# A one-core transformer block: values in 128-token matmuls, swapped by small DMAs, and a new written-out order

## The chip, the cores and the metric

The kernel runs on one core of one Trainium2 chip. Its time is the device time of one execution, in microseconds, and the profile's span is the time from the first to the last instruction of one profiled execution. Engines are named as in the profile: PE is TensorE (PEld its weight loads), DVE VectorE, ACT ScalarE, POOL GpSimd, and SP the engine that issues nearly all DMAs.

## The reference

Activations x are 2048 tokens by 512 features, in bfloat16. A conditioning vector c (1 x 512) gives, by `silu(c) @ w_mod`, six modulation vectors of 512 (sa, ca, ga, sb, cb, gb). Then:

```
h = layernorm(x) * (1 + ca) + sa
x = x + ga * attention(h)              # 32 heads of 16; a token sees itself and the 255 before it
h = layernorm(x) * (1 + cb) + sb
g = layernorm(h)                       # then an MLP across tokens, not features:
u = gelu(g^T (512 x 2048) @ w1 (2048 x 1792) + b1)
x = x + gb * (u @ w2 (1792 x 2048) + b2)^T
```

## The kernel before, in words

**Tiles and groups.** The tokens are 16 tiles of 128 (`xres`), worked on in four groups G of 512 tokens. For each group `proj` normalizes x (`norm_ops`, `normalize`), transposes it to h1T (features on the partitions; group 0 by PE, groups 1 to 3 by DMA transposes that SP issues, line 825), applies the modulation, and makes queries, keys and values with `wqkv`. A head has only 16 features, so scores are made for 4 heads by 32 rows of PE, with two heads of one 32-row strip kept apart by zeros: GpSimd multiplies each key tile twice with a parity mask (`kk`, KT).

**Chunks.** `attention(group)` runs over 75 chunks of at most 512 score columns for each of four row strips. One chunk is scores (S, on PE, into the PSUM tiles `pss` of three banks and `psb` of one), two exponentials on ACT (EA of 1536 columns, EB of 512, into `et`), a mask on DVE, and then, by units of 256 queries, AV: et times the values VT, and et times ones for the denominators. ACT takes the logarithm and exponential of the denominators (`lz`), DVE multiplies (`OT`). Group 0 has chunks 0 to 14, the others 20 each.

**Values.** VT holds, per block of 64 tokens and per head, 64 + 64 partitions by 32 columns: even heads' values on the first 64 partitions in the first 16 columns, odd heads' on the last 64 in the last 16, zeros elsewhere. In groups 0 (line 754) and 1 to 3 (line 907) one tile of 128 tokens is two half tiles of eight matmuls. Each matmul takes 64 tokens as the weights and 256 value columns (the even or the odd heads) and writes 64 output partitions; even and odd go to different columns of PE's array, so that the result already lies on the right partitions. It is copied once to `vb` (`e_ve`), and GpSimd writes it twice into VT, each time with a half mask that makes the zeros (`e_vp`, line 938).

**First queries.** `opening` (line 671) makes the first 256 tokens' keys and queries of the first 8 heads. The keys of tokens 0 to 127 and the queries share a PSUM tile of three banks (`box["warm"]`) that earlier held warm-up matmuls and next holds the first scores; DVE and ACT read them from there (`e_split`, line 691).

**MLP.** `post` finishes a group: output projection (pa), second and third layer norm, hb. `partials` (line 1034) multiplies the first eight hb tiles (groups 0 and 1) with w1 and puts 14 partial sums aside (pu, `part`), as filler on PE; the first four parts stand in a pool of their own, the later ones in room that the projections give back. `tail` does the rest of MLP1, gelu and guT; the loop at line 1302 then makes 16 output tiles: 14 matmuls into py, one addition on DVE (`otile`), one DMA.

**What sets the order.** Every step is an `op` with an engine, a planned cost and dependencies. `ORDER` (line 59) is the order of all 1,112 steps, written out by hand as a list of numbers; `CHOSEN` says which engine takes a step that can go to more than one. `run_schedule` (line 152) emits the steps in that order; the costs only decide which of three PSUM banks (`ps_od`) a step takes. Each engine, and SP's DMA queue, then works strictly in its own part of that order, and semaphores do the waiting. Since all goes through the recording class at line 225, nearly every instruction in the profile has line L233, and they are told apart by their tiles.

Of the kernel before, what the change touches and what calls it, by code (L numbers as in the profile page):

```python
# [25 lines left out]
NPART = 14  # L26
PART_AT = 20.0
# [3 lines left out]
X_READY = [3.0, 3.6, 11.8, 12.2]  # L31
MOD_READY = [4.7, 5.4, 6.2, 6.9]
W_READY = [8.1, 8.95, 8.95, 11.4, 13.6]
# [20 lines left out]
SWITCH = 0.095  # L54
LATENCY = {"PE": 0.18, "ACT": 0.15, "DVE": 0.13, "POOL": 0.15, "SP": 0.0}
# [4 lines left out]
    38, 3, 1, 9, 39, 4, 10, 11, 2, 12, 40, 13, 7, 0, 41, 6, 14, 16, 42, 17, 43, 44, 45, 18, 46, 47, 19, 8, 20, 5,  # L60
    48, 49, 51, 50, 52, 53, 55, 54, 56, 69, 57, 70, 121, 71, 122, 73, 72, 74, 58, 75, 79, 76, 123, 125, 59, 80, 77,
    126, 84, 81, 78, 85, 82, 83, 127, 129, 88, 60, 86, 130, 61, 87, 62, 63, 66, 124, 64, 67, 89, 65, 68, 133, 90,
    131, 92, 134, 259, 93, 91, 105, 94, 106, 260, 135, 137, 107, 97, 95, 138, 261, 98, 108, 96, 262, 139, 161, 110,
    99, 162, 263, 111, 109, 101, 132, 163, 140, 165, 102, 166, 112, 136, 141, 114, 142, 264, 103, 143, 169, 167,
    115, 128, 144, 100, 116, 170, 145, 146, 481, 120, 147, 151, 117, 148, 266, 179, 15, 171, 152, 119, 149, 168, 21,
    268, 267, 180, 22, 482, 113, 150, 269, 153, 23, 183, 181, 27, 118, 154, 28, 184, 265, 155, 24, 270, 182, 156,
    172, 104, 157, 185, 271, 29, 193, 25, 158, 164, 194, 30, 186, 31, 26, 159, 32, 197, 195, 173, 273, 160, 198,
    174, 483, 175, 187, 272, 188, 176, 201, 199, 484, 189, 177, 202, 485, 274, 178, 703, 275, 278, 203, 276, 211,
    279, 212, 704, 281, 280, 282, 277, 204, 190, 215, 213, 285, 283, 216, 286, 200, 284, 289, 214, 191, 196, 319,
    217, 290, 192, 287, 320, 205, 486, 705, 293, 488, 487, 37, 321, 323, 291, 206, 324, 288, 36, 207, 297, 218, 298,  # L70
    706, 208, 327, 325, 294, 299, 328, 300, 219, 295, 220, 209, 33, 337, 35, 329, 221, 210, 338, 34, 301, 707, 330,
    927, 489, 302, 225, 222, 303, 341, 339, 928, 226, 322, 223, 342, 228, 224, 229, 340, 490, 326, 304, 343, 230,
    351, 292, 305, 352, 227, 234, 306, 331, 237, 353, 492, 355, 231, 356, 354, 296, 232, 238, 235, 929, 344, 357,
    359, 236, 332, 360, 307, 493, 333, 233, 308, 239, 309, 361, 369, 491, 708, 334, 311, 310, 370, 312, 240, 345,
    313, 241, 371, 373, 346, 335, 494, 374, 930, 347, 336, 315, 495, 316, 375, 383, 348, 503, 317, 384, 242, 504,
    358, 496, 314, 362, 349, 387, 385, 497, 350, 505, 388, 363, 376, 244, 364, 365, 372, 931, 389, 391, 506, 498,
    507, 366, 392, 390, 500, 318, 709, 243, 501, 393, 401, 246, 502, 508, 367, 402, 386, 377, 710, 378, 509, 379,
    245, 712, 403, 405, 511, 380, 368, 406, 510, 404, 932, 519, 394, 512, 407, 415, 713, 520, 513, 499, 416, 250,
    395, 396, 521, 417, 419, 714, 408, 381, 397, 420, 515, 382, 248, 247, 516, 421, 249, 423, 517, 933, 523, 398,
    424, 251, 526, 527, 422, 715, 524, 425, 528, 433, 522, 399, 711, 426, 434, 409, 410, 525, 411, 400, 412, 529,  # L80
    252, 437, 435, 530, 438, 418, 531, 253, 427, 514, 532, 428, 439, 541, 436, 413, 429, 440, 542, 533, 414, 254,
    534, 716, 537, 430, 535, 545, 543, 538, 431, 546, 441, 432, 442, 540, 717, 443, 544, 257, 547, 539, 549, 447,
    444, 548, 550, 255, 448, 450, 256, 449, 451, 551, 559, 459, 536, 718, 445, 560, 719, 446, 452, 453, 552, 561,
    258, 563, 456, 460, 564, 457, 518, 720, 454, 458, 565, 573, 553, 455, 574, 554, 461, 733, 575, 462, 577, 734,
    578, 566, 463, 722, 735, 723, 579, 581, 724, 725, 582, 576, 555, 580, 726, 562, 583, 591, 464, 727, 737, 556,
    592, 738, 584, 466, 567, 739, 593, 595, 465, 568, 557, 596, 729, 558, 468, 467, 569, 721, 597, 472, 605, 730,
    606, 469, 740, 473, 470, 570, 609, 607, 731, 741, 728, 610, 474, 585, 586, 471, 571, 613, 736, 611, 587, 572,
    594, 614, 755, 475, 742, 476, 588, 623, 615, 598, 756, 624, 744, 757, 745, 616, 599, 625, 627, 589, 600, 628,
    479, 590, 601, 612, 747, 480, 608, 629, 746, 637, 748, 477, 602, 630, 638, 617, 626, 478, 618, 749, 619, 639,
    743, 641, 631, 603, 632, 642, 604, 633, 935, 732, 620, 645, 643, 936, 621, 937, 646, 622, 758, 938, 640, 940,  # L90
    644, 647, 939, 655, 941, 656, 648, 750, 942, 943, 657, 659, 649, 634, 658, 660, 650, 944, 651, 751, 635, 763,
    661, 636, 752, 764, 662, 946, 753, 947, 948, 652, 754, 765, 767, 949, 653, 768, 663, 654, 664, 950, 665, 769,
    771, 669, 666, 770, 772, 670, 672, 671, 673, 667, 781, 773, 668, 951, 674, 782, 678, 766, 679, 774, 675, 783,
    785, 680, 676, 786, 681, 952, 784, 775, 677, 787, 795, 776, 796, 788, 777, 759, 682, 760, 778, 799, 797, 953,
    761, 762, 800, 954, 683, 957, 955, 958, 801, 803, 684, 779, 956, 789, 804, 790, 802, 685, 791, 780, 959, 934,
    805, 813, 792, 962, 806, 814, 963, 798, 960, 964, 793, 686, 961, 817, 815, 965, 818, 794, 688, 687, 807, 808,
    966, 690, 809, 819, 827, 816, 973, 694, 828, 974, 689, 968, 969, 810, 829, 691, 831, 970, 811, 832, 971, 812,
    820, 975, 976, 695, 833, 835, 692, 830, 821, 836, 972, 822, 823, 693, 977, 979, 824, 696, 980, 978, 837, 845,
    825, 981, 846, 826, 982, 834, 945, 891, 838, 984, 847, 983, 849, 892, 850, 985, 893, 894, 986, 697, 851, 859,
    895, 852, 698, 860, 839, 897, 840, 896, 841, 861, 863, 842, 987, 898, 864, 990, 988, 991, 700, 992, 843, 989,  # L100
    865, 867, 701, 995, 868, 866, 993, 699, 967, 848, 996, 994, 997, 899, 702, 877, 862, 869, 853, 900, 878, 854,
    870, 855, 844, 998, 901, 879, 881, 1001, 880, 882, 999, 1002, 1003, 902, 1004, 883, 871, 856, 884, 1013, 1000,
    1005, 872, 857, 873, 885, 858, 874, 886, 904, 875, 887, 1035, 888, 876, 1006, 903, 889, 1007, 890, 1008, 905,
    1009, 909, 906, 910, 1010, 912, 911, 1028, 1011, 913, 915, 1021, 1056, 914, 1012, 1036, 1049, 916, 1063, 1014,
    908, 917, 907, 1029, 918, 1022, 919, 1057, 1042, 920, 1043, 922, 1015, 1044, 921, 1037, 1023, 923, 1064, 1030,
    924, 1050, 926, 1016, 925, 1051, 1058, 1017, 1038, 1018, 1024, 1045, 1019, 1025, 1031, 1065, 1026, 1032, 1070,
    1020, 1077, 1033, 1039, 1052, 1059, 1046, 1040, 1091, 1027, 1071, 1053, 1047, 1066, 1078, 1034, 1041, 1098,
    1054, 1060, 1084, 1072, 1055, 1061, 1067, 1092, 1073, 1079, 1074, 1105, 1048, 1099, 1068, 1080, 1085, 1081,
    1075, 1086, 1062, 1100, 1069, 1082, 1087, 1076, 1093, 1088, 1094, 1101, 1089, 1095, 1106, 1083, 1107, 1096,
    1102, 1108, 1090, 1103, 1109, 1097, 1110, 1104, 1111,  # L110
]
CHOSEN = {
    "ACT": [
        46, 49, 65, 71, 1005, 1010,
    ],
    "DVE": [
        47, 48, 50, 51, 68, 73, 76, 78, 81, 83, 86, 90, 94, 96, 99, 103, 107, 109, 112, 114, 117, 119, 243, 245, 247,
        272, 276, 280, 283, 287, 291, 295, 299, 303, 306, 310, 313, 317, 465, 467, 469, 471, 494, 495, 498, 502, 505,
        509, 513, 517, 521, 525, 528, 532, 535, 539, 687, 689, 716, 717, 720, 724, 727, 731, 735, 739, 742, 746, 749,
        753, 757, 761, 939, 944, 950, 955, 961, 966, 972, 977, 983, 988, 994, 999,  # L120
    ],
    "POOL": [
        249, 273, 691, 693,
    ],
}
BATCH = True
XT_AFTER = 1.3
W1_AFTER = 4.0
AV_POS = 0.2
LZ_POS = 0.0  # L130
M_POS = -0.5
# [60 lines left out]
def kernel(  # L192
# [381 lines left out]
    def normalize(e, dst, src, key, i):  # L574
        _, mv, rs, nm = box[key]
        if nm is None:
            ENGINE[e].tensor_scalar(
                out=dst, in0=src, scalar1=mv[:, i, 0:1], scalar2=rs[:, i : i + 1], op0=ALU.subtract, op1=ALU.mult,
            )
        else:  # L580
            ENGINE[e].tensor_scalar(
                out=dst, in0=src, scalar1=rs[:, i : i + 1], scalar2=nm[:, i : i + 1], op0=ALU.mult, op1=ALU.add,
            )


    k_done, q_done, v_done = {}, {}, {}
    proj_last = {}
    score_ops, av_ops, mult_ops = {}, {}, {}
    x_landed = [2.9, 3.5, 3.6, 4.2]
    rings = {}  # L590

# [756 lines left out]
```

## Time and profile before

| | |
|---|---|
| median of 3 runs | 257.95 us (257.77 to 258.38) |
| the profiled execution | 258.97 us |
| its span | 257.2 us |
| granted PE clock | 1.00 |
| bytes read from HBM, written | 22.03 MB, 2.10 MB |

The page gives each engine's busy share, then the span in 40 slices of 6.4 us with a digit of busy tenths for each; the digit 9 stands for 90% or more. A group of instructions is one operation with its tiles, written as out<-in, and its shapes (partitions x elements); behind the bar are its busy time, the mean duration of one in ns, and the idle time of the engine just before it with what ended it. In the views in order of time a line is: start, length, engine, operation, tiles, and in brackets the idle time before it. Matmuls overlap in PE's pipeline: the time that one costs is the distance of starts, not its duration.

### The profile page before, as it was taken

To read this page: it belongs to the slowest core of one execution; us is meant where nothing else is said; L and a number is where in the kernel's file an instruction comes from. 1 tells how busy PE (TensorE), PEld (TensorE's weight loads), DVE (VectorE), ACT (ScalarE), POOL (GpSimd) and SP (SyncE) were. 2 spreads that over 40 slices of the span, in tenths; PEclk is the share of its full clock that TensorE was granted. 3 is DMA by queue.
4 is the path that set the end of the run, shared out by engine and by line. 5 is a ranking of instruction groups with operands and counts; after the bars stand their busy time and mean duration, and the time that the engine had idled before them with its cause. 6 is when DMAs were issued, how large, how long until landed. Compare 5 with 4: busy or idle time off the path is not lost. (4 is left out here: it accounts for less than half of the span.)

```text
span 257.2 us, 8252 instructions
## 1 busy us (share of the span) xinstructions
PE 236.8 (92%) x3520; PEld 125.6 (49%) x3557; DVE 201.9 (78%) x388; ACT 180.0 (70%) x254; POOL 127.6 (50%) x212
## 2 busy tenths in 40 slices
PE   8889899999988899879999998999999999999994
PEld 2646555544655444445554544445444444444441
DVE  5599989999999999999557879888868864444443
ACT  4499999999999799999999998997237510000000
POOL 5158979998999995887950198270000000000000
PEclk9999999999999999999999999999999999999999
DMA  6999430265982000000030133023999101111111
GB/s 214 321 351 260 42 48 4 43 166 71 291 132 47 4 3 3 3 3 5 3 84 0 32 110 111 3 84 106 363 388 386 68 22 41 43 53 49 42 43 41
DMA packets 39278, 26.25 MB, mean 102 GB/s; under 512 B 11592, under 2 KB 35144, under 8 KB 39240
## 3 DMA queue, kind: packets, MB, share of 16 engines
q1 hardware_dynamic: 38944, 25.18, 35.0%
q8 instruction: 28, 0.46, 0.8%
q10 hardware_dynamic: 296, 0.53, 0.6%
q14 instruction: 10, 0.08, 0.1%
HBM read 22.03 MB, written 2.10 MB: 94 GB/s over the span
## 5 line engine op out<-in xcount | busy, mean ns | idle before, releaser
L233 ACT ACTIVATE et<-pss 128x1536 bf16<-128x1536 f32 x75 | 110.3, 1470 | 3.0 <-PE psb L233 1.7
L233 PE MATMUL pu<-hb,w1p 128*128 128x512 bf16 x214 | 51.4, 380 | 1.5 <-DVE part L233 0.7
L233 DVE TENSOR_TENSOR et<-et,maskt 128x1024 bf16<-128x1024 bf16 (+2 forms) x79 | 48.3, 634 | 4.3 <-ACT et L233 4.1
L233 PE MATMUL py<-guT,w2r 128*128 128x512 bf16 x219 | 48.1, 379 | 0.2
L233 ACT ACTIVATE et<-psb 128x512 bf16<-128x512 f32 x75 | 46.6, 622 | 0.0
L233 PE MATMUL pss<-QT,KT 32*128 32x64 bf16 (+3 forms) x720 | 30.0, 230 | 6.6 <-ACT et L233 5.3
L233 PEld LDWEIGHTS <-w2r 128*128 128x128 bf16 x224 | 21.9, 98 | 26.4
L233 PE MATMUL po<-et,VT 128*32 128x64 bf16 (+3 forms) x960 | 32.1, 234 | 2.3 <-DVE kb L233 1.2
L233 PEld LDWEIGHTS <-w1p 128*128 128x128 bf16 x224 | 20.4, 98 | 25.8 <-issue 3.0
L233 POOL TENSOR_SCALAR KT<-kb,mask_par 128x512 bf16<-128x512 bf16 (+1 forms) x38 | 27.2, 728 | 8.9 <-ACT kb L233 7.7
L233 PE MATMUL po<-et,ones_bd 128*32 128x256 bf16 (+3 forms) x624 | 31.4, 268 | 0.0
L233 DVE TENSOR_TENSOR otile<-py,xr 128x512 bf16<-128x512 f32 x16 | 11.1, 692 | 25.3 <-PE py L233 23.7
L233 PEld LDWEIGHTS <-KT 32*128 32x128 bf16 x960 | 16.6, 92 | 28.6 <-issue 26.2
L233 PE MATMUL psb<-QT,KT 32*128 32x64 bf16 (+3 forms) x240 | 29.4, 231 | 0.0
L233 POOL TENSOR_SCALAR VT<-vb,mask_half 128x512 bf16<-128x512 bf16 x32 | 26.6, 841 | 4.9 <-DVE vb L233 4.9
L233 PEld LDWEIGHTS <-VT 128*32 128x32 bf16 x960 | 19.3, 96 | 13.1 <-issue 11.4
L233 POOL TENSOR_SCALAR xn<-x,rs,nm 128x512 bf16<-128x512 bf16 x24 | 23.2, 969 | 0.8 <-DVE h L233 0.4
L233 DVE BATCH_NORM_STATS2 st<-x 128x6 f32<-128x512 bf16 x32 | 21.8, 684 | 1.9 <-DMA x<-in_A_x_dram 1.7
L233 PE MATMUL pk<-h1T,wqkv 128*128 128x256 bf16 (+2 forms) x102 | 20.1, 316 | 1.7 <-DVE OT L233 0.7
L233 PEld LDWEIGHTS <-wqkv 128*128 128x128 bf16 x164 | 13.5, 97 | 14.1 <-issue 7.4
L233 PE MATMUL pv<-wqkv,h1T 128*64 128x256 bf16 x256 | 18.7, 277 | 0.3 <-DVE part L233 0.2
L233 DVE TENSOR_TENSOR OT<-po,lz 128x256 bf16<-128x256 f32 x32 | 13.3, 415 | 6.8 <-ACT lz L233 6.8
(98 smaller groups left out, 307.4 us busy)
## 6 DMA issues: line engine op xcount, KB each, us to landing
w1p<-in_B_w_dram SPq DMA_DIRECT2D x14, 512.0 KB, 5.1
w2r<-in_B_w_dram SPq DMA_DIRECT2D x14, 512.0 KB, 9.5
x<-in_A_x_dram SPq DMA_DIRECT2D x16, 128.0 KB, 5.4
wmod<-in_w_mod_dram SPq DMA_DIRECT2D x4, 512.0 KB, 7.4
out_dram<-otile SPq DMA_DIRECT2D x16, 128.0 KB, 1.7
wqkv<-in_A_wqkv_dram SPq DMA_DIRECT2D x4, 256.0 KB, 5.8
wmod<-in_w_mod_dram ACTq DMA_DIRECT2D x2, 256.0 KB, 4.1
wmod<-in_w_mod_dram SPq DMA_DIRECT2D x2, 256.0 KB, 5.0
```

Of the source, the lines that this page charges most:

```text
L233: ins = call(*args, **kwargs)
```

## The change

In words:

- **Values of groups 1 to 3.** Four matmuls of 128 tokens by 512 columns instead of sixteen of 64 by 256; all heads' values of a token then lie on that token's partition. `vb` is written with even and odd heads sorted apart. Half of it lies on the wrong 64 partitions; two DMAs of 64 x 256 values, issued by SP, move it to a new tile `vs`. GpSimd copies four pieces of 64 partitions into VT, without masks. The zeros are written once, by two GpSimd memsets of the two VT buffers that group 0 does not use. The third buffer is group 0's, whose masked form leaves zeros in it, and group 3 uses it again.
- **First queries** get a PSUM bank of their own from the three of `ps_od`.
- **Last output tile.** Its 14 matmuls, addition and DMA are done in two halves of 256 columns.
- **PART_A = 3**: three instead of four parts stand in the pool that is there early.
- **A new ORDER and CHOSEN.** By PE's instruction list the chunks keep their order; what stands between them moves by a chunk here and there, and after chunk 53 hardly at all. In the opening, four of the eight first transposes stand ahead of the second modulation matmul, and six instead of four warm-up matmuls follow the modulation. Two h1T go from ACT to DVE, two query copies from DVE to ACT, one part from DVE to ACT.
- Planned costs, readiness times and latencies are retuned; SP's planned latency is 2.0 in place of 0, and steps that are no transfer get extra=-2.0. They issue nothing.

```diff
+PART_A = 3
-SWITCH = 0.095
-LATENCY = {"PE": 0.18, "ACT": 0.15, "DVE": 0.13, "POOL": 0.15, "SP": 0.0}
+SWITCH = 0.107
+LATENCY = {"PE": 0.18, "ACT": 0.15, "DVE": 0.13, "POOL": 0.15, "SP": 2.0}
...
+    zeros = [
+        op("z", {"POOL": 2.2, "DVE": 1.15}, 2.2, lambda e, r=r: ENGINE[e].memset(VT[r][:], 0.0), pos=2.0 * r) for r in (1, 2)
+    ]
...
             def e_qm():
+                box["q0"] = bank([P, 2 * P], F32, "pq")
                 for dc in range(ND):
                     te.matmul(
-                        box["warm"][:, 2, 0 : 2 * P], lhsT=wqkv[:, dc, 0:P], rhs=h1T[:, dc, cols],
+                        box["q0"][:], lhsT=wqkv[:, dc, 0:P], rhs=h1T[:, dc, cols],
...
-            q = op("qe", "DVE", 0.35, lambda e: ve.tensor_copy(out=QT[0][0][:, cols], in_=box["warm"][:, 2, 0 : 2 * P]), deps=[z], pos=pos)
+            q = op("qe", "DVE", 0.35, lambda e: ve.tensor_copy(out=QT[0][0][:, cols], in_=box["q0"][:]), deps=[z], pos=pos)
...
             def e_v(n):
                 if n == 0:
-                    box["v", tb] = bank([P, 2, 256], F32, "pv")
-                pv = box["v", tb]
-                wv = wqkv[:, :, 2 * D : 3 * D].rearrange("p j (a two d) -> p j two a d", two=2, d=DH)
-                tok = slice(tb * P + n * KB, tb * P + (n + 1) * KB)
-                for dc in range(ND):
-                    for par in range(2):
-                        te.matmul(
-                            pv[KB * par : KB * (par + 1), n, :].rearrange("p (a d) -> p a d", d=DH),
-                            lhsT=h1T[:, dc, tok], rhs=wv[:, dc, par, :, :],
-                            start=(dc == 0), stop=(dc == ND - 1), tile_position=(0, KB * par),
-                        )
+                    box["v", tb] = bank([P, D], F32, "pv")
+                for dc in (2 * n, 2 * n + 1):
+                    te.matmul(
+                        box["v", tb][:], lhsT=h1T[:, dc, tb * P : (tb + 1) * P], rhs=wqkv[:, dc, 2 * D : 3 * D],
+                        start=(dc == 0), stop=(dc == ND - 1),
+                    )
...
+                copy(
+                    e, vb[:].rearrange("p two (a d) -> p a two d", d=DH),
+                    box["v", tb][:].rearrange("p (a two d) -> p a two d", two=2, d=DH),
+                )
+
+            def e_vx(e):
+                vs = box["vs", tb] = work.tile([P, 256], BF, name="vs", tag="vs")
+                dma.dma_start(out=vs[0:KB, :], in_=box["vb", tb][KB:P, 0, :])
+                dma.dma_start(out=vs[KB:P, :], in_=box["vb", tb][0:KB, 1, :])
 
             def e_vp(e):
                 for half in range(2):
-                    place(e, box["vb", tb][:], half)
+                    rows = slice(KB * half, KB * half + KB)
+                    for block, src in ((half, box["vb", tb][rows, half, :]), (1 - half, box["vs", tb][rows, :])):
+                        po.tensor_copy(
+                            out=VT[r3][rows, 2 * tb + block, :, half * DH : (half + 1) * DH],
+                            in_=src.rearrange("p (a d) -> p a d", d=DH),
+                        )
...
+            vx = op("vx", "SP", 0.85, e_vx, deps=[ve_op], pos=pos)
+            b = op("vp", "POOL", 1.75, e_vp, deps=[vx] + war + zeros, pos=pos)
...
-                part[fc] = box["A" if fc < 4 else "B"].tile([P, D], F32, name=f"part{fc}")
+                part[fc] = box["A" if fc < PART_A else "B"].tile([P, D], F32, name=f"part{fc}")
...
-        for n, fc in enumerate(order):
-            te.matmul(
-                py[:], lhsT=w2r[tb // 8][:, fc, tb % 8 * P : (tb % 8 + 1) * P], rhs=guT[fc][:],
-                start=(n == 0), stop=(n == NF - 1),
-            )
         ot = gtmp.tile([P, D], BF, name="otile")
-        ve.tensor_tensor(out=ot[:], in0=py[:], in1=xr[:], op=ALU.add)
-        dma.dma_start(out=out_dram[tb * P : (tb + 1) * P, :], in_=ot[:])
+        for cols in (slice(0, D),) if tb < NT - 1 else (slice(0, D // 2), slice(D // 2, D)):
+            for n, fc in enumerate(order):
+                te.matmul(
+                    py[:, cols], lhsT=w2r[tb // 8][:, fc, tb % 8 * P : (tb % 8 + 1) * P], rhs=guT[fc][:, cols],
+                    start=(n == 0), stop=(n == NF - 1), skip_group_check=True,
+                )
+            ve.tensor_tensor(out=ot[:, cols], in0=py[:, cols], in1=xr[:, cols], op=ALU.add)
+            dma.dma_start(out=out_dram[tb * P : (tb + 1) * P, cols], in_=ot[:, cols])
```

## The prediction

> **What bounds the kernel now.** I read the page's shares and slices first, then the busy times by stretch, then the instructions in order of time, and the groups by shape.
>
> ```profile
> PE 236.8 (92%) x3520; PEld 125.6 (49%) x3557; DVE 201.9 (78%) x388; ACT 180.0 (70%) x254; POOL 127.6 (50%) x212
> ...
> ACT  4499999999999799999999998997237510000000
> ```
>
> TensorE leads over the whole span, but ScalarE is full from the second slice to the 24th. The stretches separate the two (start:end and length, then busy us and instructions of PE, PEld, DVE, ACT and POOL, granted clock, DMA share, GB/s):
>
> ```profile
> 12.00:20.00 8.00, 6.72 (x100) 4.52 (x99) 7.65 (x18) 7.36 (x12) 4.40 (x9) 1.00 1.09 351
> 20.00:40.00 20.00, 17.88 (x428) 11.75 (x428) 18.82 (x42) 19.99 (x29) 17.59 (x28) 1.00 0.52 102
> ...
> 80.00:100.00 20.00, 16.96 (x320) 8.99 (x320) 19.59 (x35) 18.70 (x26) 18.99 (x26) 1.00 0.05 9
> 100.00:120.00 20.00, 16.78 (x390) 9.62 (x388) 19.28 (x35) 19.82 (x26) 14.59 (x25) 1.00 0.01 3
> ...
> 182.00:254.00 72.00, 71.33 (x326) 32.40 (x331) 42.10 (x79) 12.39 (x19) 0.00 (x0) 1.00 0.35 125
> ```
>
> From 12 to 124 us the exponentials on ScalarE set the pace (75 chunks of about 1.94 us, 32 units of about 0.57), with VectorE at 95 to 98% and, from 27 to 98 us, GpSimd near 95%: TensorE waits there. From 124.21, where the first partial product of MLP1 starts, TensorE has filler and is the bound to 253.9. So a saving has three prices: TensorE time before 124 is nearly worthless; an earlier or denser exponential stream is worth its full length, since all later work moves with it; TensorE time after 124, and the last output, count in full.
>
> **Part 1, first queries in their own bank, and the new order of the opening.**
>
> ```profile
> 9.29 0.39 PE L233 MATMUL pk<-h1T,wqkv 128*128 128x128 bf16 x4
> 10.15 0.60 PE L233 MATMUL pss<-h1T,wqkv 128*128 128x256 bf16 x4 [0.48 <-DVE KT L233]
> ...
> 12.00 1.45 ACT L233 ACTIVATE et<-pss 128x1536 bf16<-128x1536 f32 x1
> ...
> 18.24 1.02 ACT L233 ACTIVATE h1T<-pt,modFM 128x256 bf16<-128x256 bf16 x2 [0.61 <-PE pt L233]
> ```
>
> The first is the wait that goes: the queries shared the bank that VectorE was still splitting the first keys from. With an own bank TensorE runs keys, queries, keys, scores without that 0.48. Next late is the h1T that the keys need. In the new order the first transposes stand ahead of the second modulation matmul, whose weights land at 6.65; the last of those weights still land at 7.37, so only some 0.14 is won. First exponential: 12.00 - 0.48 - 0.14 = 11.38.
>
> ScalarE's own queue then changes (instruction lists of both kernels side by side): the two h1T of 18.24 go to VectorE, with their 0.61 of idle (0.91 to the next instruction, so 1.52), and two query copies come (0.34 each, from the 0.38 kb copy and its successor; 0.68). By the seventh chunk the stream is ahead by 0.62 + 1.52 - 0.68 = **1.46**. VectorE gains two h1T (0.33 each) and loses the two copies (0.33 each): nothing. The transposes that fed those h1T also come after the third score chunk rather than between value tiles, and VectorE's first xn stands behind three copies instead of five. Bounds: 0.48 if ScalarE merely waits elsewhere, 2.1 if its other small waits close too.
>
> **Part 2, values.** Per tile sixteen 64-column matmuls become four of 512 columns, with 12 tiles in groups 1 to 3. From starts in the timeline: eight old ones between AV and scores take 46.83 to 47.39 = 0.56, two dense ones before AV 68.57 to 69.10 = 0.53. So 0.03 a half tile, 24 halves, 0.7 us. Also, a change between the kinds of matmul costs about 0.097: a dense 512 starts 0.215 before the next dense one, 0.312 before a score. Counted in the two instruction lists there are 205 changes before and 192 after; but between partials and the end only 57 and 55. Since TensorE waits before 124, only the last four halves (0.12) and these two changes (0.19) count: **0.3**. Of the remaining 0.6 + 1.1 I take **0.3**, for the places where ScalarE waited for scores (2.1 us in all from 45 to 124); bounds 0 and 1.7. [...]
>
> What the values pay for it:
>
> ```profile
> L233 POOL TENSOR_SCALAR VT<-vb,mask_half 128x512 bf16<-128x512 bf16 x32 | 26.6, 841 | 4.9 <-DVE vb L233 4.9
> ...
> L233 POOL TENSOR_SCALAR KT<-kb,mask_par 128x256 bf16<-128x256 bf16 x14 | 6.5, 476 | 8.7 <-ACT kb L233 7.7 <-DVE kb L233 1.0
> ...
> L233 POOL COPY maskt<-tmpm 64x64 bf16<-64x64 bf16 x6 | 1.3, 248 | 0.0
> ...
> L233 POOL MEMSET tmpm<- 128x256 bf16 x1 | 0.3, 316 | 0.1
> ```
>
> GpSimd: two TENSOR_SCALAR (1.68) become four copies of 64 partitions x 256 elements. A copy lies between the 64-element COPY (0.248) and the 512-element TENSOR_SCALAR (0.841); nearest is the 256-element one, 0.476, and I take 0.45, so 1.8: +0.12 a tile, bounds -0.7 and +1.7. Eight tiles fall before 100 us: +1 us on a queue that has no slack of its own there, but whose products have: the fourth value tile of group 1 is in place at 60.97 and first read at 63.32 (2.35), the later ones by more, and GpSimd idles 4.2 us between 98 and 118 before the second group's last norm (hb, done 124.12). So nothing, at 0.45.
>
> The DMAs: 24 of 32 KB. Nearest rows: a 128 KB output lands 1.7 us after issue, an h1T transpose 2.7. I take 2.2 (bounds 1.7 and 5.1, the w1p row). The route of each tile is longer by that, but today group 1's fourth tile leaves TensorE at 50.5 and GpSimd reaches it only at 58.92, and in the new order its matmuls stand a chunk (2.2) earlier. On SP's queue the pairs stand among the transposes and the w1 loads; about 0.5 each to issue, as the opening's loads. Behind the pairs of group 1 stand the transposes of group 2, behind group 2's fourth the last transpose of group 3 (issued at 80.89 now, after a value tile of 79.77 to 80.8): no later than today. The w1 loads have 45 us. VectorE's copy keeps its 512 elements from PSUM (0.678); the reordered output I take as free, bounds 0 and 0.1 each.
>
> Zeros: two memsets of 4096 elements ahead of all keys. From 128 elements in 204 ns and 256 in 316, 0.875 ns an element: 3.68 each; bounds 1.9 (half, if two values go at once) and 5.1 (316 ns per 256). GpSimd is free from 4.5 to 12.21, so with the masks (2.4) it is done at 2.04 + 2 x 3.68 + 2.4 = 11.8. The second unit's keys are ready for it at 11.1, must start by 12.5 for the second exponential (14.05: the copy and the norm's two logs now precede it), so 0.7 is left. Nothing, but see the rivals.
>
> **Part 3, last output tile.** Same columns: twice 14 x 0.109 (256 columns, 8 in 0.97 with a change) for 14 x 0.216. After TensorE's end:
>
> ```profile
> 253.90 0.69 DVE L233 TENSOR_TENSOR otile<-py,xr 128x512 bf16<-128x512 f32 x1 [1.67 <-remote]
> ```
>
> The last addition has 256 elements, 0.41 as OT and kb have: **0.28**. Landing (1.69) and closing (0.94) stay; at best 0.15 from half the bytes.
>
> PART_A = 3 delays the fourth partial to the end of the projections; that one starts behind them anyway. Retimed constants only move bank choices and the order.
>
> **Sum.** 1.46 + 0.3 + 0.3 + 0.28 = 2.35 off the profiled span, 257.2 to 254.9. That execution took 258.97, 1.0 above the median of the runs shown; the same saving on the median gives 257.95 - 2.35 = **255.6**.
>
> **Rivals.**
> 1. *VectorE takes the place of ScalarE's wait.* For: 18.8 to 19.6 of 20 busy from 20 to 120, and its work does not shrink. Against: it idles 2.3 us between 11.5 and 45, and 1.9 just before. Then only the 0.48 at the start, the tail and a little stay: 257.95 - 0.9 = 257.0, or within 0.2% if GpSimd adds to it. Chance 0.18.
> 2. *GpSimd becomes the bound; slower.* Place: values of groups 1 and 2 (45 to 98 us). It decides when six tiles' surplus exceeds 2.35 + the 2.2 of the earlier matmuls, 0.76 a tile, a copy of 0.61. At 0.84 the surplus is 10 us, 5.5 over: 255.6 + 5.5 = 261; at 0.7, about 258.3. For: the same shapes run from 0.68 to 1.47 in the trace, the long ones beside VectorE's masks. Against: the uncontended 256-element row is 0.47. Chance 0.17. [...]
> 3. *Zeros are too long.* At 5.1 each the keys start at 14.6, the second exponential is 2.1 late: 257.95 - 0.2 = 257.7, no change. Chance 0.07.
> 4. *More than forecast:* TensorE's shorter queue also removes the stalls at 80 to 87 us (ScalarE 1.3 idle) and others before 124: 253.8. Chance 0.13.
> 5. *The change does not do what it says:* the own bank is another bank whose holder frees it late, so the 0.48 wait returns; 256.1, inside the forecast.
>
> **How the numbers follow.** Forecast (254.5 to 256.8) 0.45; rivals 0.18, 0.17, 0.07 and 0.13. Eight in ten: from 253.6, which takes in rival 4, to 258.8, which leaves out the heavy end of rival 2. About 0.2% (0.5 us) is what a measurement here can tell from no change. Faster: 0.45 + 0.13 + 0.13 of rival 1 = 0.71; same 0.05 + 0.05 = 0.10; slower 0.17 + 0.02 = 0.19.
>
> **What would show it.** First exponential at 11.3 to 11.5, no DVE KT wait before the pq matmuls, fourth exponential near 18 (now 19.63): part 1. First pu near 122.4 (now 124.21), with hb complete by then: the stream carried it. VT copies near 0.45, memsets near 3.7, vs landing in 2 to 3, no AV waiting for POOL VT: part 2. Last addition 0.41: part 3. It is wrong if KT or VT on GpSimd releases scores or AV for more than about 1 us in sum, or if pu starts no earlier.

## The result, and the profile after

The changed kernel takes 264.13 us (263.96 to 264.75, 4 runs) against 257.9 for the kernel before: ratio 1.0242, 95% interval 1.0221 to 1.0264. The forecast was 255.6, in a range of 253.6 to 258.8; it was slower, not faster. The profiled execution took 263.96, its span is 262.2. The page's lines that answer to those of the prediction, with the clock's:

```profile
PE 236.4 (90%) x3388; PEld 122.6 (47%) x3427; DVE 202.9 (77%) x388; ACT 179.7 (69%) x255; POOL 137.6 (52%) x238
...
ACT  4269999999899999999999999997137520000000
...
PEclk9989999999999999999999999999999999999999
```

Busy time does not explain 6 us: TensorE's is 0.4 lower than before, ScalarE's and VectorE's are the same to 1, and GpSimd's 10 more are half of its span away from a bound. What is new is a 2 and a 6 in ScalarE's second and third slice, and an 8 in the clock. The stretches, with the columns of the prediction:

```profile
12.00:20.00 8.00, 7.62 (x97) 5.26 (x95) 5.36 (x15) 5.49 (x11) 3.02 (x7) 0.79 1.10 350
20.00:40.00 20.00, 17.28 (x341) 11.17 (x343) 19.40 (x42) 19.99 (x28) 17.07 (x28) 1.00 0.46 98
80.00:100.00 20.00, 17.25 (x377) 9.35 (x379) 18.47 (x36) 19.41 (x28) 18.14 (x30) 1.00 0.12 26
```

From 12 to 20 us ScalarE works 5.49 instead of 7.36, and TensorE is busier than before, 7.62 against 6.72, with fewer instructions: its clock is 0.79. The loss lies there first. In order of time, from the start:

```profile
2.04 3.52 POOL L235 MEMSET VT<- 128x4096 bf16 x1
2.97 0.70 DVE L235 BATCH_NORM_STATS2 st<-x 128x6 f32<-128x512 bf16 x1 [1.07 <-DMA x<-in_A_x_dram]
...
7.51 4.13 DVE L235 TENSOR_SCALAR h1T<-h1T,modFM 128x256 bf16<-128x256 bf16 x3
...
8.01 3.55 POOL L235 MEMSET VT<- 128x4096 bf16 x1
...
11.69 0.38 PE L235 MATMUL pss<-h1T,wqkv 128*128 128x128 bf16 x4 [3.17 <-DVE h1T L235]
...
15.48 1.45 ACT L235 ACTIVATE et<-pss 128x1536 bf16<-128x1536 f32 x1 [0.17 <-PE psb L235]
```

In the kernel before, the same two places are:

```profile
8.27 0.86 DVE L233 TENSOR_SCALAR h1T<-h1T,modFM 128x256 bf16<-128x256 bf16 x3
...
8.67 0.78 PE L233 MATMUL pss<-h1T,wqkv 128*128 128x128 bf16 x4
```

Three multiplies of h1T took 0.86 us before and take 4.13 here; they end at 11.64, 0.08 after the second memset of zeros. VectorE counts as busy all the while, so no list of waits shows the stall: it is a duration to be held against its own duration before. TensorE waits 3.17 for h1T, and the first exponential comes at 15.48, where 11.38 was forecast and 12.00 was before. The first keys start 3.02 later than before (11.69 against 8.67) and the new bank wins 0.64 behind them (see e12); that leaves 1.1 of the 3.48, and it is the clock:

```profile
12.00:13.00 1.00, 1.00 (x11) 0.75 (x9) 0.61 (x2) 0.63 (x2) 0.00 (x0) 0.57 1.10 347
13.00:14.00 1.00, 1.00 (x6) 0.74 (x5) 0.78 (x2) 0.00 (x0) 0.00 (x0) 0.50 1.09 347
14.00:15.00 1.00, 1.00 (x13) 0.48 (x14) 0.97 (x3) 0.07 (x1) 0.00 (x0) 0.50 1.10 348
15.00:16.00 1.00, 1.00 (x18) 0.54 (x11) 0.23 (x2) 0.83 (x2) 0.58 (x2) 0.73 1.10 350
```

For 3.41 us behind its idle stretch of 3.17 TensorE is granted half its clock. In other runs it came behind shorter waits too (2.7 and 2.19, last section).

A second loss stands near 66 us. The waits of the whole span, the DMA ones (engine and tile, what it waited for, us in total, times, longest):

```profile
POOL VT L235 <- DMA vs<-vb: 6.8, 4, 3.3
...
DVE h1T L235 <- DMA vs<-vb: 2.4, 1, 2.4
```

The view of the tile vs gives the time from issue to landing of the 24 small transfers:

```profile
DMA to landing us min/median/max: 1.7/1.9/6.4
```

The median (1.9) is even below the 2.2 forecast, the longest (6.4) is far above. In order of issue, on SP's queue:

```profile
56.23 2.83 SPq L1023 DMA_DIRECT2D w1p<-in_B_w_dram  x3
59.15 1.82 SPq L933 DMA_DIRECT2D vs<-vb  x1
```

The fourth pair of group 1 (issued at 59.15 and 61.01) and the transpose behind it (61.71) landed between 65.5 and 66.1, with three 512 KB loads of w1 in front of them that were issued from 56.23 to 57.51 and landed at 61.19, 62.93 and 65.29. VectorE's wait of 2.4 ended at 66.16, just behind the landing of that transpose (66.08); the list puts it down to vs. GpSimd's groups by shape (busy us, mean ns, then the idle time before them and its releaser) put these 6.8 beside the size of the copies and memsets:

```profile
L235 POOL COPY VT<-vb 64x256 bf16<-64x256 bf16 x24 | 12.3, 513 | 2.4 <-DVE vb L235 1.7
L235 POOL COPY VT<-vs 64x256 bf16<-64x256 bf16 x24 | 11.2, 466 | 6.8 <-DMA vs<-vb 6.8
...
L235 POOL MEMSET VT<- 128x4096 bf16 x2 | 7.1, 3534 | 0.1
```

The third loss is at the end, again in order of time:

```profile
257.51 1.69 PE L235 MATMUL py<-guT,w2r 128*128 128x256 bf16 x14 [0.52 <-DVE otile L235]
...
259.24 0.42 DVE L235 TENSOR_TENSOR otile<-py,xr 128x256 bf16<-128x256 f32 x1 [1.78 <-PE py L235]
```

The last addition is 0.42 as forecast, but the second half's matmuls first wait 0.52 for the addition that reads the first half.

To place losses along the span I compare when ScalarE starts the first exponential of a chunk, in the profiled executions. The experiments' columns are explained below. The profiled execution of before is 1.0 slower than its median, and that of e12 (256.35) is the fastest of its twelve, so a lead over the column of before can be up to 1.0 too large.

| start, us | before | after | e5 | e9 | e12 |
|---|---|---|---|---|---|
| chunk 0 | 12.00 | 15.48 | 11.20 | 11.48 | 10.62 |
| chunk 24 | 64.59 | 68.42 | 62.69 | 62.71 | 62.96 |
| chunk 36 | 92.08 | 94.44 | 88.25 | 88.84 | 89.80 |
| chunk 72 | 169.43 | 172.79 | 166.86 | 167.18 | 167.13 |
| first output matmul | 205.35 | 209.98 | 203.98 | 203.44 | 203.05 |
| end of span | 257.25 | 262.25 | 255.73 | 255.02 | 254.64 |

### The profile page after: what moved, and what is told of

The parts are those of the page before. It is cut to its first block, busy times and chain, and to the rows that moved or that the text cites. A ratio compares the mean times of both kernels' runs of the same rounds, so it can differ in the third digit from the quotient of the medians.

```text
span 262.2 us, 8080 instructions
## 1 busy us (share of the span) xinstructions
PE 236.4 (90%) x3388; PEld 122.6 (47%) x3427; DVE 202.9 (77%) x388; ACT 179.7 (69%) x255; POOL 137.6 (52%) x238
## 4 chain that ended last, share of the span: by engine, by line
PE 42%; DVE 16%; POOL 13%; ACT 10%; issue 5%; DMA 3%; DVEq 0%; POOLq 0%
PE py L235 18%; PE pu L235 15%; ACT et L235 8%; DVE et L235 3%; POOL KT L235 3%; PE po L235 3%; POOL xn L235 3%; DVE h L235 3%; PE pss L235 3%; DMA vs<-vb 2%; PE pa L235 2%; DVE st L235 2%; POOL VT L235 2%; ACT lz L235 2%; POOL sq L235 2%
## 5 line engine op out<-in xcount | busy, mean ns | idle before, releaser
L235 PE MATMUL py<-guT,w2r 128*128 128x512 bf16 (+1 forms) x234 | 48.5, 366 | 0.7 <-DVE otile L235 0.5
L235 PEld LDWEIGHTS <-w2r 128*128 128x128 bf16 x238 | 23.3, 98 | 26.0 <-issue 0.7
L235 DVE TENSOR_TENSOR otile<-py,xr 128x512 bf16<-128x512 f32 (+1 forms) x17 | 11.2, 661 | 25.7 <-PE py L235 24.0
L235 POOL TENSOR_SCALAR KT<-kb,mask_par 128x512 bf16<-128x512 bf16 (+1 forms) x38 | 26.4, 707 | 7.6 <-ACT kb L235 3.9
L235 PEld LDWEIGHTS <-VT 128*32 128x32 bf16 x960 | 19.6, 96 | 16.8 <-issue 14.9
L235 PE MATMUL pk<-h1T,wqkv 128*128 128x256 bf16 (+2 forms) x102 | 20.9, 328 | 1.3 <-DVE OT L235 0.7
L235 PEld LDWEIGHTS <-wqkv 128*128 128x128 bf16 x164 | 14.1, 101 | 17.0 <-issue 9.6
L235 PE MATMUL pv<-wqkv,h1T 128*64 128x256 bf16 (+1 forms) x108 | 16.6, 318 | 1.1 <-DVE OT L235 0.9
L235 PE MATMUL pa<-wod,OT 128*128 128x512 bf16 x60 | 16.3, 380 | 0.8 <-DVE OT L235 0.5
```

Source lines behind the costliest of these rows:

```text
L235: ins = call(*args, **kwargs)
```

## The experiments

Fourteen kernels ran, each beside the kernel before (its median was 258.1 to 258.4 in these sessions). Theory: GpSimd's memset holds VectorE, the loads of w1 hold the small transfers, the shared tile holds the last half. Rivals stand with each.

| | us | ratio to before, 95% interval |
|---|---|---|
| e1_split | 260.12 | 1.0064 (1.0041 to 1.0086) |
| e2_before_zeros | 262.34 | 1.0160 (1.0133 to 1.0186) |
| e3_own_bank | 263.04 | 1.0185 (1.0159 to 1.0211) |
| e4_w1_late | 261.64 | 1.0130 (1.0091 to 1.0169) |
| e5_all_three | 257.88 | 1.0004 (0.9975 to 1.0033) |
| e6_old_values | 264.35 | 1.0227 (1.0180 to 1.0275) |
| e7_values_alone | 263.69 | 1.0192 (1.0145 to 1.0239) |
| e8_fill | 264.16 | 1.0215 (1.0162 to 1.0269) |
| e9_old_values_late | 256.41 | 0.9937 (0.9922 to 0.9953) |
| e10_values_alone_late | 267.05 | 1.0365 (1.0341 to 1.0389) |
| e11_old_end | 257.56 | 0.9997 (0.9972 to 1.0022) |
| e12_bank_halves | 257.18 | 0.9964 (0.9952 to 0.9976) |
| e13_late_fill | 264.13 | 1.0208 (1.0166 to 1.0250) |
| e14_shift | 260.03 | 1.0078 (1.0050 to 1.0106) |

**e1, memsets in pieces.**

```diff
-lambda e, r=r: ENGINE[e].memset(VT[r][:], 0.0)
+lambda e, r=r: [ENGINE[e].memset(VT[r][:, n], 0.0) for n in range(8)]
```

> The changed kernel with each of the two zero memsets cut into 8 pieces of 512 elements (about 0.44 us each); everything else as changed. Theory (GpSimd's memset holds VectorE out while it runs, so a 3.5 us piece of GpSimd work is a 3.3 us wait of VectorE): the multiply of h1T starts within 0.5 us of its operands, first EA at 11.5 to 12.5 instead of 15.48, no stretch of granted clock at 0.5, total 259.5 to 261.0. If the pieces leave VectorE no gap between them the wait stays, and the total with it (264). Rival (the first scores wait for something else, and the memset only happens to end then): nothing moves, 264.

```profile
7.75 1.14 DVE L235 TENSOR_SCALAR h1T<-h1T,modFM 128x256 bf16<-128x256 bf16 x3
...
8.24 3.91 POOL L235 MEMSET VT<- 128x512 bf16 x8
```

In order of time again: GpSimd works just as long (3.91), and VectorE gets in between two pieces: 1.14 instead of 4.13. First exponential 11.23, clock 1.00 throughout (in the profiled execution), 260.12. So it is the length of one GpSimd instruction that costs, not GpSimd's time.

**e2, the memsets alone, in the kernel before.** Two lines in `emit_masks`, ahead of the masks and behind them:

```diff
+        po.memset(VT[1][:], 0.0)
         po.memset(tmpm[:], 1.0)
...
+        po.memset(VT[2][:], 0.0)
```

> The kernel before with the same two memsets of the value tiles added at the places that the change gives them on GpSimd, though nothing in it needs them; all else as before. Theory (VectorE is held out): the multiply of h1T takes 3 to 4 us longer, first EA 15 to 16 instead of 12.0, granted clock at 0.5 for some 3 us behind it, total 261.0 to 262.0 (+3.2 to +4.2). Rival (GpSimd has idle time from 4.5 to 12.2 us and hides them): 257.9, first EA 12.0.

```profile
8.10 3.51 POOL L233 MEMSET VT<- 128x4096 bf16 x1
...
8.37 3.64 DVE L233 TENSOR_SCALAR h1T<-h1T,modFM 128x256 bf16<-128x256 bf16 x3
...
16.01 1.45 ACT L233 ACTIVATE et<-pss 128x1536 bf16<-128x1536 f32 x1 [0.17 <-PE psb L233]
```

The same stall without the rest of the change, and 3.9 us more in all (262.34 against 258.41), with the clock at 0.50 from 13.4 to 16.8 us. That GpSimd was idle there was no cover. The lag of 4.0 at chunk 0 is still 3.3 at chunk 72.

**e3, the second half in its own tile.**

```diff
+        py2 = box["ps_t"].tile([P, D], F32, name="py2", tag="pst3") if tb == NT - 1 else None
...
+            if cols.start:
+                py = py2
```

> The changed kernel with the second half of the last output tile in a PSUM tile of its own. Theory (the matmuls of the second half wait for the addition that reads the first half out of the same tile, 0.52 us): this wait goes, total 263.5 (-0.5 to -0.6). Rival (the wait is the engine's own drain between two accumulation groups): nothing moves, 264.1.

The wait went. From the first output matmul to the end of the span it takes 51.58 us, after 52.27, before 51.90. The 0.69 is a little more than the wait; the 0.32 against before is what the halved tile was forecast to bring. The median fell by 1.1, more than this explains; the runs of e3 spread over 1.1.

**e4, the loads of w1 late.** The seven steps w1l stand behind the last transpose in ORDER, and a tiny memset on GpSimd holds each:

```diff
+        if half == 0:
+            po.memset(t[:, 0, 0:2], 0.0)
         dma.dma_start(out=t[:], in_=w1_v[...])
```

> The changed kernel with the seven 512 KB loads of w1 held back, by a memset of two columns on GpSimd ahead of each, to behind the last transpose of h1T (about 94 us); all else in the same order. Theory (the small transfers of the values and one transpose queue behind these loads): no vs transfer takes over 3 us, VectorE's wait at 66 us (2.4) and GpSimd's at 65.6 (2.0) go, total 262.6 to 263.1 (-1.0 to -1.5). Rival (the stream of scores has slack there and gives it back later): below 0.3 us of change.

The longest small transfer takes 3.8 instead of 6.4 (under 3 was expected), VectorE's wait at 66 us is gone, and the lag behind the kernel before at chunk 27 is 2.71 instead of 4.40. GpSimd still waits 4.5 in two places. The total fell by 2.5, more than the 1.5 expected, but the executions differ: two of 262.96 and 262.13 with a mean clock of 0.993, two of 260.88 and 261.15 at 1.000. In the first kind the loads are worth 1.2 to 2.0; the step from 262.5 to 261.0 is a first measure of the half clock, 1.5.

**e5, all three repairs.** 

> The changed kernel with all three repairs: memsets in 8 pieces, loads of w1 behind the last transpose, second half of the last tile in its own PSUM tile. Theory (the three losses stand one behind the other on the path and add up: 4.0 of the memsets, 1.0 to 2.5 of the loads, 0.5 of the tile): 257.0 to 258.6, within 0.5% of the kernel before on either side. Rival (the losses hide one another, so that the second repair gives little): 259.0 to 260.0.

257.88: together the three are worth 6.25, and the kernel is where the kernel before is. By the traces they were worth 4.0 (e1), 1.3 (e4, the lag at chunk 72 down from 3.36 to 2.03) and 0.7 (e3), 6.0 in all: they hide next to nothing of one another, and the rival is out.

**e6, the old values in the new order.** `v` and its steps as before, ORDER without the steps of zeros and transfers. 

> The changed kernel with the values of groups 1 to 3 made as in the kernel before (64 tokens per matmul, no small transfers, no zero memsets), and the new order, the own bank of the first queries and the halved last tile kept. Theory (the new values' zeros, transfers and their queue are what costs; the order itself is sound): first EA near 11.3, no wait at 66 us, total 257.6 to 259.0, so the form of the values is worth under 1 us by itself. Rival (the new order needs the shorter value matmuls): scores fall behind by the longer value matmuls in the middle, 260 or more.

```profile
DVE h1T L234 <- DMA h1T<-xn: 6.3, 1, 6.3
ACT et L234 <- PE psb L234: 5.4, 1, 5.4
PE po L234 <- DVE QT L234: 5.1, 1, 5.1
```

The expectation failed: 264.35. These are the waits from 56 to 68 us, one behind the other: VectorE waits 6.3 for a transpose issued at 57.20 that landed at 64.80. Without the small transfers SP had put five loads of w1 ahead of it, issued from 50.55 on. Half the clock follows, from 63.6 to 70.4. So the loads strike what lies behind them; in this edit it is another transfer than in after.

**e7, the values alone in the old order.** `v` as in the change, zeros in pieces, ORDER of before with the transfers behind their copies:

```diff
-vs = box["vs", tb] = work.tile([P, 256], BF, name="vs", tag="vs")
+vs = box["vs", tb] = hb[14 + tb % 2][:, 0:256]
```

> The kernel before, in its own order, with only the values of groups 1 to 3 made as in the change (zeros in 8 pieces at the same places of GpSimd; the halves that change places lie in columns of output tiles 14 and 15 that are not used until later, as there is no room for them otherwise). Theory (the matmuls of the values become shorter and GpSimd's copies cost no more than the old placing): 257.3 to 258.5, a gain of 0 to 0.6. Rival (GpSimd stands still for each small transfer, 2 us and more behind the loads of w1, and what is queued behind it comes late): 259.5 to 262.

The rival was right, 263.69. From 76 to 92 us:

```profile
POOL VT L234 <- DMA hb<-vb: 6.7, 2, 3.5
ACT et L234 <- PE pss L234: 5.2, 1, 5.2
PE pk L234 <- DVE vb L234: 3.8, 1, 3.8
DVE vb L234 <- POOL VT L234: 3.8, 1, 3.8
```

Read from below: VectorE can't copy the next tile because GpSimd has not yet emptied the buffer, GpSimd waits for a transfer, TensorE waits for VectorE's copy, ScalarE for scores. The two waits were for a pair behind the loads (landed at 76.74, 3.4 after its issue) and for a pair that took the plain 1.8. So in the old order even a pair that takes no longer than usual is waited for.

**e8, idle time of TensorE filled.** Ahead of the first keys:

```diff
+                for i in range(13):
+                    te.matmul(box["warm"][:, 1, :], lhsT=warm[:, 0:P], rhs=warm[:], start=True, stop=True)
+                e_k(0)
```

> The changed kernel with 13 more matmuls of zeros on TensorE between the warm-up and the first keys, which fill the 3.2 us in which it waits for VectorE; the memsets and the wait stay. Theory (the idle stretch lowers the granted clock to 0.5 for 3.4 us behind it, which costs about 1.6 us): no stretch at 0.5, total 262.2 to 263.0. Rival (at half the clock the scores still keep ahead of ScalarE): 264.

In the profiled execution the clock stays at 1.00, the first exponential comes at 13.98 (1.50 earlier than after), and the gain holds to chunk 21 (1.48). Then all is given back between chunks 36 and 39, 8.84 us apart instead of 7.11: VectorE waits 2.8 for a transpose of h1T, where it waits 0.9 in after. The total, 264.16, so tells nothing of the clock, although it is the rival's number; see e13 and the last section.

**e9, old values, late loads, own tile.** e6 with the edits of e3 and e4; it differs from e5 in the values alone. 

> The kernel e6 (the new order with the values as before) with two of the repairs more: the seven loads of w1 behind the last transpose, and the second half of the last tile in its own PSUM tile. It differs from e5 in the form of the values alone. Theory (e6 lost its 5.4 us between chunks 21 and 24 to a transpose that queued behind five loads of w1, and to the half clock after it, and not to the form of the values): 257.0 to 258.6, within 0.6 of e5. Rival (the new order can't do with the longer value matmuls): 260 or more.

256.41, the fastest kernel here, 0.63% faster than before; that is below the expected 257.0, and 1.5 from e5 where 0.6 was expected. The rival is out: the new order needs no new values. They are a loss of 1.5 by the medians, though their matmuls are shorter:

```profile
L234 PE MATMUL pv<-wqkv,h1T 128*64 128x256 bf16 x256 | 17.6, 276 | 0.5 <-DVE OT L234 0.3
```

In e5 these are 12.3 + 4.3 = 16.6 busy us, but its trace lacks 4 of the 48 long ones. By the distances of starts, idle time taken off, those of groups 1 to 3 take 12.5 in e9 and 11.8 in e5. By the table e5 is 0.3 ahead at chunk 0, level at chunk 24 and 0.3 ahead at chunk 72: the shorter matmuls bring at most 0.3 on the path. Then e5 loses 0.85 before the first output matmul.

**e10, e7 with the loads behind the values of group 2.** 

> The kernel e7 (the kernel before in its own order, with the values of the change) with the seven loads of w1 held back to behind the last values of group 2. Theory (e7 lost its 4.9 us between chunks 30 and 33 to GpSimd's wait for transfers of 32 KB, and the first of these waits came of the loads): 258.0 to 259.0. Rival (the wait for a 2 us transfer alone, with GpSimd's queue behind it, is enough in an order made for the old placing): 261 to 263.5.

The theory falls: 267.05. The loss between chunks 30 and 33 shrank from 4.9 to 2.3, but a new one of 4.9 stands between 48 and 51: four transfers of group 3, issued from 115.59 on behind the loads that I had moved, landed at 121.3 to 121.9, and GpSimd waited 6.4 for them. In the old order I found no place for these 3.6 MB that is not ahead of some small transfer.

**e11, e5 with the order of before behind the last scores.** 

> The kernel e5 (all three repairs) with the order of the kernel before for everything behind the last scores. Theory (of the new order's 1.1 us between chunk 72 and the output matmuls, 0.6 is TensorE's wait for a bank of the attention sums and the rest leftover work): 256.9 to 257.6. Rival (that work is only moved): 257.9.

257.56 is within the theory's range but no change from e5 that can be told, and from chunk 72 to the first output matmul it is 37.2 as in e5 (37.1), as the rival said. The order of the end is not what costs. What does, in order of time on TensorE in e5:

```profile
174.73 0.39 PE L235 MATMUL po<-et,ones_bd 128*32 128x256 bf16 x7
175.70 0.27 PE L235 MATMUL po<-et,ones_bd 128*32 128x256 bf16 x1 [0.58 <-issue]
```

TensorE stands 0.58 in the middle of the attention sums and waits for nothing that the profile shows. e1, e5 and e11 have this among the same 104 matmuls (0.58 to 0.69), and so have after (0.72), e3 (0.32), e4 (0.80), e8 (0.77) and e13 (0.76); before, e9 and e12 do not. In e5 and e11 the profile names nothing that ends it, in after VectorE's OT. In e8 and e13, whose 13 more matmuls and weight loads shift TensorE's program by 26 instructions, it comes 13 matmuls earlier in the row (in after it comes behind the 3,037th weight load of the trace): it keeps its place in the program, not in the work.

**e12, two parts alone in the kernel before:** the own bank of the first queries, and the halves with a tile each. 

> The kernel before, with its own order and values, and two parts of the change done alone: the first queries in a bank of their own, and the last output tile in two halves, each in its own PSUM tile. Theory (each is worth what the prediction gave it): first EA 0.4 to 0.5 earlier, end of the last output 0.3 earlier, 257.3 to 257.7. Rival (the first 0.5 us is taken up again by the stream of scores): 257.9 to 258.2.

257.18, faster than before by 0.36%. From the first pk matmul to the first scores it is 1.63 (8.55 to 10.18), before 2.27: 0.64 gained. The first exponential is 1.38 earlier, but 0.74 of that lie ahead of the keys, where loads arrive. From the first output matmul to the end it is 51.59 (before 51.90): 0.31 gained, as the prediction had it.

**e13, e8 with the loads late.** 

> The changed kernel with the loads of w1 behind the last transpose (as e4) and the 13 fill matmuls of zeros of e8; the memsets and VectorE's wait for them stay. In e8 the 1.5 us that the fill saved were given back at 96 us, where a transpose came 1.1 us late; here the work stands elsewhere. Theory (the idle stretch of TensorE costs the granted clock, and that costs 1.5 us by itself): 260.4 to 261.4, all runs near those two of e4 (260.9, 261.2) whose mean granted clock was 1.000. Rival (the half clock is hidden and the gain of e8 is always given back): 262.1 to 263.0, like the two runs of e4 at 0.993.

The stream is 1.3 ahead of e4 up to chunk 36 (91.60 against 92.88). Then the same transpose wait of 2.8 takes it: 264.13, with one execution of six at 260.78, where the theory put all. Four of the six have a mean clock of 0.993 or 0.994, and so have three of the four of e8 (0.992 or 0.993); one stretch of 3.41 at half clock gives 0.993, so there the collision seems to bring a half clock of its own. So the half clock costs 1.3 to 1.5 in the stream, and what e13 shows beside is a collision that the fill brings with it.

**e14, e5 with TensorE's program shifted by 32 instructions.**

```diff
-            te.matmul(box["warm"][:, i, :], lhsT=warm[:, 0:P], rhs=warm[:], start=True, stop=True)
+            for m in range(17 if first and i else 1):
+                c = slice(0, 8) if first and i else slice(0, D)
+                te.matmul(box["warm"][:, i, c], lhsT=warm[:, 0:P], rhs=warm[:, c], start=True, stop=True)
```

> The kernel e5 (all three repairs) with one of its warm-up matmuls at the start replaced by 17 small ones of 8 columns, so that every later instruction of TensorE stands 32 places further back in its program, at the place that it has in e9 but for 256. Theory (the 0.6 us for which TensorE stands still in the attention sums near 175 us, released by nothing that the profile shows, comes of where its program is cut into the pieces that are loaded): the stand goes, and the stretch from chunk 72 to the first output matmul is 36.3 to 36.6 us instead of 37.1, total 257.1 to 257.4. Rival (it comes of the kernel's data or banks): 37.1 us and 257.9.

The stand is gone and the stretch is 36.28, as the theory said; the total is not, 260.03. The shift brought the wait of e8 and e13 (3.3 at 92 us) and a half clock from 96.2 to 99.6 behind it: against e5 it loses 2.7 us between chunks 36 and 39, and 3.6 by chunk 48.

## Why the prediction was wrong

**The step that failed first** is in part 2: "Zeros: ... Nothing, but see the rivals." The size was right (3.68 forecast, 3.53 measured, both done at 11.56 against 11.8). What failed is the question: I asked whether GpSimd's own queue would be late, and not whom a long GpSimd instruction holds. The price is 4.0 us (e1), 3.9 by e2, wait and clock together. Rival 3 had the zeros, but by another mechanism (memsets of 5.1 us that make GpSimd's keys late) and at 2.1 us. Rival 2 had the right pair of engines (GpSimd's 0.68 to 1.47 for the same shapes, the long ones beside VectorE's masks) and used it one way only, with GpSimd as the one that waits. The memset does not hold all that VectorE does: the multiplies take 4.13 beside it, the statistics under the first memset 0.70 at 2.97, like everywhere (mean 0.68). By what it holds the multiplies no run shows.

**The second** is "no later than today. The w1 loads have 45 us." The loads have that time; what queues behind them has not. Landing was bounded at 5.1 and measured 6.4. Price 1.2 to 2.5 (e4). That an order is tight where it was planned for other transfers is the wider lesson of e6, e7 and e10, 2 to 4% slower than before by one or two such waits each.

**The third** is part 3's "0.28". The addition is right (0.42 for 0.41), but two halves of one PSUM tile wait for each other: 0.7 lost against e3, which does gain the 0.3.

**The fourth** is the gain of the values, 0.3 + 0.3. TensorE's value matmuls did get shorter, by 0.6 (forecast 0.7), but on the path little of it is seen: e5 is level with e9 at chunk 24, at most 0.3 ahead at chunk 72, where 0.6 was forecast, and 0.5 behind at the first output matmul. In place of a gain the form of the values cost 1.5 by the medians (1.3 when each is held against the kernel before in its own session), of which 0.6 is the stand that e14 removes by moving the program. The other 0.9 is open: by the profiled executions e5 and e9 differ by 0.7 only.

**What held.** Part 1: the wait of 0.48 went, 0.64 in e12, and with the repairs the stream is ahead by 1.89 at the seventh chunk (e5; forecast 1.46; a part of this lead can be the slow execution of before). Rivals 1 and 2 stayed away: GpSimd's four copies take 1.96 a tile (1.8 forecast), 0.49 each, under the 0.61 from which it would decide. (At a copy of 0.7 rival 2's own sum gives 6 x 1.12 - 4.55 = 2.2 over the forecast, 257.8, not 258.3.) Without the values the forecast would have been 255.6 + 0.6 = 256.2; e9, which is that kernel with the repairs, takes 256.4.

So the sum: 255.6 + 4.0 + 2.2 for loads and tile (e5 against e1) + 1.5 for the values (e5 against e9) + 0.6 that was never there = 263.9; measured 264.13. The first three terms behind 255.6 are differences of measured medians, so of the forecast the sum tests only its rest, 256.2 against 256.4.

## What to carry to other kernels

Before a long instruction is put on an idle engine, look at which other engine's instructions run at that time, and hold their durations against those before; cut it into pieces of the length that the neighbour can wait (here the multiplies took 4.13 beside one memset of 3.55, 1.14 beside eight of 0.49). A small transfer that something waits for costs its place in the queue, not its size (32 KB landed 1.7 to 6.4 us after issue): read what was issued before it, megabytes included, and again after every edit. When a change is made of parts, run the parts: here the two that were sound (e12, and the order in e9) were worth 0.4 to 0.6% and were hidden under one that was not.

## What the runs showed of the hardware

- A duration can be a wait. VectorE's three multiplies of 256 elements took 0.86, 4.13 and 1.14 us beside nothing, a 3.55 us memset and eight of 0.49, and counted as busy throughout.
- A stall of TensorE costs more than itself: half the clock for 3.41 us came behind waits of 3.17 (after), 2.7 (e14, for OT) and 2.19 us (e10, from 117.4), not behind those of 2.24 (e8 and e13, in the profiled executions). The length of one wait does not settle it: another such stretch of e10 (from 83.2) follows 3.41 us in which TensorE worked 1.58 and never waited over 1.39. The price in the stream was 1.3 to 1.5 in e8 and e13.
- A transfer can be late together with a packet that is not data. The page of after counts 27 packets of 16 KB of the kind instruction on one queue (0.44 MB); each takes 0.88 to 1.48 us. From the issue of the last transpose to VectorE's multiply it is 2.62 to 2.66 in after, e1, e3, e4, e5 and e11, and 4.45, 4.16 and 4.66 in e8, e13 and e14; in these three such a packet ended at 95.02, 93.49 and 91.02, and the multiply started 1.2 to 1.3 after. In the records of single packets the last of the transpose's own, three of 256 bytes in e13, five in e14 and two of 4 bytes in e8, come only within 0.13 us of the end of that packet. In the other six all are done 2.2 after the issue and such a packet starts later (in after at 95.64, 0.33 behind them). All three move TensorE's program, by 26 or 32 instructions. That these packets load the program and hold the transpose up is a reading; it was not tried by itself.
- Where TensorE's program lies can cost time by itself: the stand among short matmuls (0.58 in e5) moved with a shift of 26 instructions (e8, e13) and went with one of 32 (e14). Why it goes with the one and not the other is open.
